# Block 1's channel-mixing MLP: upward products first, downward in seven products per pair, its gelu kept in memory, and a new order

## Chip, core and metric

One core of one Trainium2 chip runs the kernel. The metric is the device time of one execution in microseconds, the median of several runs. Before the change it was 502.88 us (three runs, 502.44 to 503.21). All data are float32; matrix operands are kept as two rounded parts, high and low (`hi`, `lo`), and a product is made of three matrix products: high by high, high by low, low by high.

## What is computed

The input `x` has 2048 rows of 512. It is normalised, goes through linear attention with 32 heads (`A`) and, separately, through a mixer block (`B`: a spatial-shift token mixer, then an MLP with 1376 hidden columns), and the result is `x + s * silu(B)`.

```python
def _A_ref(x, wqkv, wo):
    qkv = (x @ wqkv).reshape(B, S, 3, H, Dh).transpose(2, 0, 3, 1, 4)
    q, k, v = qkv[0], qkv[1], qkv[2]
    phi = lambda t: jnp.where(t > 0, t + 1, jnp.exp(t)) + 1e-6
    pq, pk = phi(q), phi(k)
    kv = jnp.einsum("bhsd,bhse->bhde", pk, v)
    z = jnp.einsum("bhsd->bhd", pk)
    num = jnp.einsum("bhqd,bhde->bhqe", pq, kv)
    den = jnp.einsum("bhqd,bhd->bhq", pq, z)[..., None] + 1e-6
    return (num / den).transpose(0, 2, 1, 3).reshape(B, S, D) @ wo

def _B_ref(x, w1, w2, w3, w4):
    h = _gelu(_layernorm(x) @ w1)
    g0 = jnp.pad(h[:, :, 0*c:1*c], ((0, 0), (1, 0), (0, 0)))[:, :S, :]
    ...
    x1 = x + jnp.concatenate([g0, g1, g2, g3], axis=-1) @ w2
    return x1 + _gelu(_layernorm(x1) @ w3) @ w4

xn = _layernorm(A_x)
return A_x + _A_ref(xn, A_wqkv, A_wo) * _silu(_B_ref(xn, B_w1, B_w2, B_w3, B_w4))
```

`g0` to `g3` are the quarters of `h`, shifted by +1, -1, +2 and -2 rows.

## The kernel before

**Tiles.** The 2048 rows are 16 tiles `i` of 128 rows, in four blocks `b` of four tiles (`QT = 4`). The hidden width 1376 is 11 pieces `f` of 128 columns, the last (`FB - 1`) of 96; the other ten go in five pairs `s` and `s + 5` (`NS = 5`).

**Seven products.** Where a product can be cut into 2 x 2 quarters, `seven` (and `down_late`) makes it of seven quarter products instead of eight, with sums and differences of quarters (`s1` to `s4` on the left, `t1` to `t4` on the right) as extra operands. The seven results are put together by evictions from PSUM: ScalarE copies one (`p1`, `p5`, `u2`), VectorE adds it to the next.

**The stages.** First key and query projections, the token mixer (`mix1`, `mix2`), and the sums of attention. Then, from about 225 us on, the MLP block by block. The upward product (by `w3`) with gelu is `up_last` and `up_pair` or `up_late`; the downward product (by `w4`) is `down` or `down_late`.

- *Blocks 0 and 1* go the plain way. `up_pair` writes the gelu twice, rounded and full, and VectorE makes the low part (`split`). `down` then adds, for each piece `f` and each of the four tiles `j`, three 512-wide products into the PSUM bank `acc{b}_{j}`. Upward and downward products of a block are woven together. `w4` is held for one block, and block 1 loads it again from memory (`load_w4`, tiles `w4_1_*`).
- *Blocks 2 and 3* are `LATE`. Their gelu stays in full in SBUF (`HF`, `HL`). After all upward products `down_forms` builds the left forms `a11, a12, s1, s2, s4, s3, a22` with their high and low parts, and `down_late` makes 7 products x 5 pairs x 3 terms of 256 columns for each of two tile pairs, and 4 x 3 for the last piece, against the right forms `W4F` (`wf`, `wu`), fetched by `fetch_w4`. The last block is `final`: its gates (`gate`) are cut finer, and its rows of `x1` are fetched ahead.

**Attention pairs.** `attends` works off tiles in pairs (`turn_q`, `forms_q`, `attend_pair`) at the points that the table `ATT` names, and leaves `so{i}` in SBUF until `gate(i)` uses it. `SUMS` names where the right forms of `w4` are built (`sums_w4`).

**What sets the order.** Every operation is recorded in a `Plan`, and `emit` then orders each engine's operations by due times that it works out, with a table of nudges (`SOONER`: operation number, quarter microseconds sooner) on top. SBUF tiles come from a pool `p` of 90 pieces of 2 KB a row; PSUM from `mm` (4 banks) and `acc` (4 banks). An operation that needs a tile waits for one to be free. Plain transfers are issued on SyncE's queue (`load`, `store`, `fetch`), accumulating ones on GpSimd's (`gather`); each queue works in order.

Of the kernel before, what the change touches and what calls it, by code (L numbers as in the profile page):

```python
# [11 lines left out]
ALU = mybir.AluOpType  # L12
AX = mybir.AxisListType

P = 128
# [381 lines left out]
def linear_attn_gated_by_mixer(  # L397
# [20 lines left out]
    QT = 4  # L418
# [6 lines left out]
    WARM = 3  # L425
    PIECE = BT + W
    EARLY = (), (10, 0, 5, 1, 6, 2)
    LATE = 2, 3
    SUMS = {(2, 2): (3,), (2, 3): (4,)}
    ATT = {(0, 4): (0,), (0, 5): (2,), (1, 2): (4,), (1, 3): (6,), (1, 4): (8,), (1, 5): (10,), (2, 1): (12,), (2, 3): (14,)}  # L430
    AHEAD = 100.0, 90.0, 70.0, 30.0, 10.0
    TH = BT // 2
    EDGE = 64
# [77 lines left out]
    g = nc.gpsimd  # L511
# [545 lines left out]
    GROUPS = ((0, 1), (2, 3), (4,))  # L1057
    HLEFT = (("a11", "a12"), ("s1", "s2"), ("s4", "s3"), ("a22",))
    QLEFT = (("a11", "a12"), ("a21", "a22"))
    TLEFT = (("t1", "t2"), ("t3", "t4"))  # L1060
    wtd = {}
    AF3, W4, YT, H3, HF, HL = {}, {}, {}, {}, {}, {}
# [186 lines left out]
    def up_last(b):  # L1249

        f, n = FB - 1, LASTW
        y = YT[b]
        ge = piece(f"gf{b}_{f}")
        late = b in LATE
        if late:
            HL[b] = ge.rows(n)
        else:
            hi, lo = rounds(f"f{b}_{f}")
        for t in range(2):
            h = t * TH, (t + 1) * TH  # L1260
            ps = bank(f"a{b}_{f}_{t}").cols(0, TH).rows(n)
            ks = y[f"b1{t + 1}"] + y[f"b2{t + 1}"]
            products(ps, [AF3["last"][c] + ks[c] for c in range(NC)])
            if not late:
                pl.act(hi.cols(*h).rows(n), ps, AF.Gelu_apprx_tanh)
            pl.act(ge.cols(*h).rows(n), ps, AF.Gelu_apprx_tanh)
        if late:
            return
        split(lo.rows(n), ge.rows(n), hi.rows(n))
        H3[b, f] = (hi, lo, n)  # L1270
# [20 lines left out]
    def up_late(b, s):  # L1291
        at = shelf(HF.setdefault(b, {}), f"h{b}_", QLEFT, "f")
        a11, a12, a21, a22 = (at(q, s)[0] for q in QS)
        ps = seven(f"{b}_{s}", (a11, a21, a22), lambda x, y: [AF3[s][x][c] + YT[b][y][c] for c in range(2)])
        for v in (a11, a21, a22):
            pl.act(v, v, AF.Gelu_apprx_tanh)
        pl.act(a12, ps, AF.Gelu_apprx_tanh)

    DF, LF = {}, {}

    def down_forms(b):

        full, rough = {}, {}
        at, fa = shelf(full, f"d{b}f_", HLEFT, "f"), shelf(rough, f"d{b}_", HLEFT)
        own = shelf(HF[b], f"h{b}_", QLEFT, "f")
        src = lambda q, g: wide(own, q, g)[0]
        w = lambda form, g: wide(at, form, g)[0]
        for form in ("a11", "a12", "s1", "s2", "s4", "s3", "a22"):
            for g in GROUPS:
                if form in ("s1", "s3"):  # L1310
                    pl.tt(w(form, g), src("a21", g), src("a22" if form == "s1" else "a11", g), ALU.add)
                elif form == "s2":
                    pl.tt(w("s2", g), w("s1", g), src("a11", g), ALU.add)
                elif form == "s4":
                    pl.tt(w("s4", g), w("s2", g), src("a12", g), ALU.add)
                v = src(form, g) if form[0] == "a" else w(form, g)
                hi, lo = wide(fa, form, g)
                rounded(hi, lo, v)
        DF[b] = {form: [fa(form, s) for s in range(NS)] for p in HLEFT for form in p}
        hi, lo = (v.rows(LASTW) for v in rounds(f"dl{b}"))  # L1320
        rounded(hi, lo, HL[b])
        LF[b] = hi, lo

# [379 lines left out]
    def attends(key):  # L1703
        for i in ATT.get(key, ()):
# [2 lines left out]
            forms_q(i)  # L1707
            attend_pair(i)
            for k in (i, i + 1):
                if k in XO:  # L1710
                    gate(k)

# [43 lines left out]
                gate(i)  # L1756
    fetch_w4()
    make_wl()
    for b in LATE:
        down_forms(b)  # L1760
        final = b == LATE[-1]
        if final:
            ahead(b)
            pl.patience = 0.0
        down_late(b, final)

    SOONER = (
# [42 lines left out]
    )  # L1810
    pl.emit(first=6.0, lead={"p": 9.0, "w": 20.0, "ab": 10.0}, reserve={"p": 8, "w": 1, "ab": 0}, window=9.0,
            ahead=6.0, table=SOONER)
# [39 lines left out]
```

## Time and profile before

| what | value |
|---|---|
| median of three runs | 502.88 us |
| the profiled execution's own time | 502.62 us |
| its span (first to last instruction) | 500.9 us |
| granted TensorE clock, mean | 1.000 |
| instructions | 9569 |
| HBM read, written | 72.47 MB, 36.06 MB |
| TensorE busy in the first 50 us | 48.82 us |
| first upward product of block 0, roughly | 225 us |
| first downward product of block 2, roughly | 440 us |
| last product | 496.3 us |

The profile is one execution. The busy shares are averages over stages. A row of the chain of waits gives start, length and what; a row of the stretches gives the busy time of each engine in it with the count of instructions; a group's row gives the number, the busy time and the mean of one in ns. In instruction rows `out<-in` are tile names; numbers at a tile's end count buffers.

### The profile page before, as it was taken

The numbers are of one execution on the slowest core, as the hardware profiler recorded it, in microseconds if no ns is written. First come the engines' busy times: TensorE is split into PE (matmuls) and PEld (weight loads), VectorE is DVE, ScalarE is ACT, GpSimd is POOL, SyncE is SP. The second block draws the span as 40 slices with busy tenths as digits, with TensorE's granted clock in tenths as the row PEclk, the third lists the DMA queues.
The fourth block names the chain that finished last, engine by engine and source line by source line (L and its number), as shares of the span: only waits on it lengthen the run. The fifth ranks groups of instructions, "written<-read, shape, count | busy, mean of one in ns | idle before, by whom it ended". The sixth has DMA issues, their size and how long they took to land.

```text
span 500.9 us, 9569 instructions
## 1 busy us (share of the span) xinstructions
PE 495.3 (99%) x3138; PEld 442.8 (88%) x3138; DVE 430.1 (86%) x850; ACT 368.0 (73%) x826; POOL 119.2 (24%) x208
## 2 busy tenths in 40 slices
PE   9999999999999999999999999999999999999996
PEld 6788778888888897899999989999989999999996
DVE  5998888789999958999899999978899785787983
ACT  5898999968696589999977855554657676856631
POOL 1384504438930232133100022000013100000320
PEclk9999999999999999999999999999999999999999
DMA  7968994999975899989978779975648937974674
GB/s 220 328 167 233 224 289 128 214 347 284 343 201 133 221 272 276 277 200 273 371 231 220 235 214 200 303 225 178 203 145 145 283 124 246 294 225 135 117 195 131
DMA packets 84345, 113.35 MB, mean 226 GB/s; under 512 B 10024, under 2 KB 37960, under 8 KB 84296
## 3 DMA queue, kind: packets, MB, share of 16 engines
q1 hardware_dynamic: 73640, 93.35, 57.2%
q0 software_dynamic: 10656, 19.40, 23.5%
q8 instruction: 24, 0.39, 0.3%
q14 instruction: 25, 0.20, 0.1%
HBM read 72.47 MB, written 36.06 MB: 217 GB/s over the span
## 4 chain that ended last, share of the span: by engine, by line
PE 94%; ACT 3%; DMA 1%; SPq 0%; DVE 0%; issue 0%; ACTq 0%
PE acc L146 12%; PE pb L146 11%; PE g L146 9%; PE h L146 9%; PE pbd L146 6%; PE pe L146 6%; PE pbx L146 5%; PE pbs L146 5%; PE pbm L146 5%; PE ped L146 3%; PE pa L146 3%; PE pex L146 3%; PE q L146 3%; PE pem L146 2%; PE pes L146 2%; PE a L146 2%
## 5 line engine op out<-in xcount | busy, mean ns | idle before, releaser
L225 POOL DMA_DIRECT2D xo<-x1d x12 | 10.6, 1067 | 186.7 <-DVE qz L201 112.6
L225 POOL DMA_DIRECT2D o<-xnd x16 | 14.0, 885 | 39.7 <-DMA w_s<-in_w 11.9
L225 POOL DMA_DIRECT2D zacc<-ke x12 | 12.3, 1028 | 31.9 <-DVE u_2l L191 9.9
L225 POOL DMA_DIRECT2D th<-in_x x14 | 12.1, 878 | 32.0 <-DVE th L201 14.3
L168 ACT ACTIVATE th<-xo 128x512 f32<-128x512 f32 (+1 forms) x16 | 9.7, 614 | 11.1 <-DVE xo L201 10.3
L225 POOL DMA_DIRECT2D xt<-nrow x16 | 15.1, 1441 | 6.0 <-DVE wt_01l L191 3.5
L191 DVE TENSOR_TENSOR ht<-h,abc 128x512 f32<-128x512 f32 x16 | 11.1, 691 | 5.6 <-PE h L146 5.4
L168 ACT ACTIVATE ht<-ht 128x512 f32<-128x512 f32 x16 | 9.9, 628 | 4.2 <-DVE ht L191 4.0
L168 ACT ACTIVATE p<-pe 128x256 f32<-128x256 f32 x20 | 7.6, 382 | 7.2 <-PE pe L146 7.1
L168 ACT ACTIVATE p<-pb 128x256 f32<-128x256 f32 x20 | 7.7, 383 | 7.2 <-PE pb L146 7.1
L196 POOL TENSOR_SCALAR w<-mv 128x4 f32<-128x4 f32 (+2 forms) x10 | 2.9, 289 | 40.0 <-ACT sq L168 39.7
L168 ACT ACTIVATE y<-o,nm,rs 128x512 f32<-128x512 f32 x16 | 12.0, 806 | 0.5 <-POOL nm L196 0.5
L168 ACT ACTIVATE u<-pb 128x256 f32<-128x256 f32 x20 | 7.7, 383 | 5.9 <-PE pb L146 5.8
L201 DVE SCALAR_TENSOR_TENSOR th<-th,so 128x512 f32<-128x512 f32 (+1 forms) x17 | 11.1, 652 | 0.8 <-ACT th L168 0.4
L168 ACT ACTIVATE sq<-o,mv 128x512 f32<-128x512 f32 x16 | 11.4, 719 | 0.1
L201 DVE SCALAR_TENSOR_TENSOR pq<-pq,rd 128x512 f32<-128x512 f32 x16 | 10.9, 682 | 0.3
L168 ACT ACTIVATE den<-den 128x32 f32<-128x32 f32 x16 | 3.6, 228 | 9.8 <-DVE den L1421 9.8
L201 DVE SCALAR_TENSOR_TENSOR qz<-pq,zb 128x512 f32<-128x512 f32 x16 | 10.8, 680 | 0.0
L168 ACT ACTIVATE gf<-gf 128x256 f32<-128x256 f32 (+1 forms) x20 | 10.5, 523 | 0.3
L1421 DVE TENSOR_REDUCE den<-qz 128x32 f32<-128x512 f32 x16 | 10.7, 676 | 0.1
L168 ACT ACTIVATE sq<-o 128x512 f32<-128x512 f32 x16 | 10.1, 630 | 0.1
L596 POOL TENSOR_TENSOR rs<-w,nhalf 128x4 f32<-128x4 f32 (+2 forms) x10 | 9.6, 962 | 0.7
(1974 smaller groups left out, 2383.5 us busy)
## 6 DMA issues: line engine op xcount, KB each, us to landing
w_s<-in_w SPq DMA_DIRECT2D x28, 256.0 KB, 5.8
x<-in_x SPq DMA_DIRECT2D x16, 256.0 KB, 5.1
xt<-in_xt SPq DMA_DIRECT2D x16, 256.0 KB, 5.7
xnd<-x SPq DMA_DIRECT2D x16, 256.0 KB, 6.0
xt<-nrow POOLq DMA_DIRECT2D x16, 256.0 KB, 8.2
pqd<-qr SPq DMA_DIRECT2D x16, 256.0 KB, 3.3
o<-xnd POOLq DMA_DIRECT2D x16, 256.0 KB, 6.0
x1d<-o SPq DMA_DIRECT2D x16, 256.0 KB, 5.8
```

Source lines behind the costliest of these rows:

```text
L146: lambda: nc.tensor.matmul(out.get(), lhs.get(), rhs.get(), start=start, stop=stop, skip_group_check=more))
L168: nc.scalar.activation(out.get(), src.get(), func, scale=get(scale), **kw)
L191: self.vec(eng, out, [a, b], lambda: self.e(eng).tensor_tensor(out.get(), a.get(), b.get(), op=op), True)
L196: lambda: self.e(eng).tensor_scalar(out.get(), a.get(), get(s1), get(s2), **kw), False,
L201: lambda: self.nc.vector.scalar_tensor_tensor(out.get(), a.get(), get(s), b.get(), op0=op0, op1=op1),
L225: lambda: self.nc.gpsimd.dma_start(out.get(), get(src), accum_op=ALU.add), mb=mb)
L596: lambda: g.tensor_tensor(out.get(), src.get(), nh.get(), op=ALU.pow))
L1421: pl.add("DVE", .6, .68, [t], [den], lambda: nc.vector.tensor_reduce(den.get(), t.get().rearrange("p (h d) -> p h d", d=DH), axis=AX.X, op ...
```

## The change

Block 1 joins the `LATE` blocks: its upward products run without the downward ones between them, and its downward product is made by `down_late`, after those of blocks 2 and 3 (`LINE = 2, 3, 1`), so that block 1 is now `final`. Since its full gelu does not stay in SBUF (`SPILL`), each finished pair of pieces is stored to memory (`hd`), as is its attention result (`sod`). `down_forms` fetches the forms `a11, a12, a22` back, and makes `s1` and `s3` by a fetch followed by an accumulating transfer of the second quarter, where blocks 2 and 3 use a VectorE addition. The reloads of `w4` for block 1 are gone. The attention pairs go at later points of the line of upward products, and the `SOONER` table is new.

```diff
-    LATE = 2, 3
-    SUMS = {(2, 2): (3,), (2, 3): (4,)}
-    ATT = {(0, 4): (0,), (0, 5): (2,), (1, 2): (4,), (1, 3): (6,), (1, 4): (8,), (1, 5): (10,), (2, 1): (12,), (2, 3): (14,)}
+    LATE = 1, 2, 3
+    SPILL = 1,
+    LINE = 2, 3, 1
+    SUMS = {(3, 1): (3,), (3, 3): (4,)}
+    ATT = {(0, 5): (0,), (1, 1): (2,), (1, 3): (4,), (2, 0): (6,), (2, 2): (8,), (2, 4): (10,), (3, 1): (12,), (3, 3): (14,)}
...
+    HN = {(q, g): 2 * k + g for k, q in enumerate(("a11", "a12", "a21", "a22")) for g in range(2)}
+    HN.update({p: 8 + k for k, p in enumerate(QLEFT)})
+    hd = {b: memory(f"hd{b}", 11 * 512) for b in SPILL}
+    sod = {i: memory(f"sod{i}") for b in SPILL for i in range(b * QT, b * QT + QT)}
...
         if late:
+            if b in SPILL:
+                put(b, 10, HL[b], n)
             return
...
         pl.act(a12, ps, AF.Gelu_apprx_tanh)
+        if b in SPILL and (s % 2 or s == NS - 1):
+            for key in [(q, s // 2) for q in QS] if s < NS - 1 else QLEFT:
+                put(b, HN[key], HF[b][key][0])
+
+    def put(b, n, v, rows=P):
+        op = pl.store(hd[b][:rows, n * 512:(n + 1) * 512], v)
+        op.patience = 10.0
+        pl.soon(op)
+
+    def slab(b, q, g):
+        if len(g) > 1:
+            n = HN[q, g[0] // 2] * 512
+            return hd[b][:, n:n + 512]
+        p = next(p for p in QLEFT if q in p)
+        o = HN[p] * 512 + p.index(q) * TH
+        return hd[b][:, o:o + TH]
...
         for form in ("a11", "a12", "s1", "s2", "s4", "s3", "a22"):
             for g in GROUPS:
                 if form in ("s1", "s3"):
-                    pl.tt(w(form, g), src("a21", g), src("a22" if form == "s1" else "a11", g), ALU.add)
+                    other = "a22" if form == "s1" else "a11"
+                    if spilled:
+                        pl.fetch(w(form, g), slab(b, "a21", g))
+                        pl.gather(w(form, g), slab(b, other, g))
+                    else:
+                        pl.tt(w(form, g), src("a21", g), src(other, g), ALU.add)
...
+                elif spilled:
+                    pl.fetch(src(form, g), slab(b, form, g))
...
+        if spilled:
+            HL[b] = piece(f"hl{b}").rows(LASTW)
+            pl.fetch(HL[b], hd[b][:LASTW, 10 * 512:11 * 512])
...
             for k in (i, i + 1):
+                if k // QT in SPILL:
+                    pl.soon(pl.store(sod[k].all, SO[k]))
...
-    for b in LATE:
+    for b in LINE:
         down_forms(b)
-        final = b == LATE[-1]
+        final = b == LINE[-1]
+        if b in SPILL:
+            for i in range(b * QT, b * QT + QT):
+                SO[i] = piece(f"sb{i}")
+                pl.fetch(SO[i], sod[i].all)
...
     SOONER = (
-        15, 27, 20, 21, 26, 2, 30, 3, 36, 10, 52, 1, 82, 2, 91, 2, 99, 4, 103, 12, 112, -14, 113, -2, 124, 10,
+        23, 8, 39, 7, 48, -50, 69, 53, 90, 10, 93, 21, 96, 20, 97, 12, 99, 9, 106, -6, 118, -9, 120, 6, 124, 8,
...
```

How the order moves, at three places. On TensorE before, inside block 1 (`acc1_*`: its downward banks; `w4_1_*`: its copy of `w4`; `f1_*`: its gelu; `pe1_1`: an upward product of its pair 1):

```order
L146 MATMUL acc1_1_4398<-w4_1_0l_4129,f1_0h_4330 128x512
L146 MATMUL acc1_1_4398<-w4_1_0h_4097,f1_0l_4400 128x512
L146 MATMUL acc1_1_4398<-w4_1_5h_4179,f1_5h_4396 128x512
L146 MATMUL acc1_3_4276<-w4_1_0l_4129,f1_0h_4330 128x512
L146 MATMUL acc1_3_4276<-w4_1_0h_4097,f1_0l_4400 128x512
L146 MATMUL acc1_1_4398<-w4_1_5l_4162,f1_5h_4396 128x512
L146 MATMUL pe1_1_4406<-yt11h_4164,w3_1_s0l_2538 128x256
L146 MATMUL acc1_2_4304<-w4_1_5h_4179,f1_5h_4396 128x512
L146 MATMUL acc1_2_4304<-w4_1_5l_4162,f1_5h_4396 128x512
```

and in the changed kernel, near the end, where block 3's last downward products (`pbd3*`) meet block 1's first (`pbd10`, `pad10`, `ped10`; `d1_*`: its left forms; `wf_*`, `wu_*`: right forms):

```order
L146 MATMUL pbd30_6533<-w4_l1h_6366,dl3h_6524 128x256
L146 MATMUL pbd30_6533<-w4_l1l_6386,dl3h_6524 128x256
L146 MATMUL pbd30_6533<-w4_l1h_6366,dl3l_6541 128x256
L146 MATMUL pbd10_6978<-wf_b111h_5829,d1_a111l_6871 128x256
L146 MATMUL pbd31_6621<-w4_l1l_6386,dl3h_6524 128x256
L146 MATMUL pbd31_6621<-w4_l1h_6366,dl3l_6541 128x256
L146 MATMUL pad10_6996<-wf_b210l_6019,d1_a120h_6954 128x256
L146 MATMUL ped10_7047<-wu_00h_6070,d1_s10h_6898 128x256
L146 MATMUL ped10_7047<-wu_00l_6079,d1_s10h_6898 128x256
L146 MATMUL ped10_7047<-wu_00h_6070,d1_s10l_6909 128x256
```

The 512-wide products of block 1 among its upward ones are gone, and 256-wide ones stand behind block 3's.

On VectorE, around the first eviction of block 1's upward stage; before (`gf1_*`: gelu input of block 1; `so`, `th`: gates of block 0; `f1_*l`: low parts; `qz`, `den`: attention):

```order
L191 TENSOR_TENSOR so2_4064<-so2_4064,xo2_4198 128x512
L191 TENSOR_TENSOR so3_4113<-so3_4113,xo3_4210 128x512
L201 SCALAR_TENSOR_TENSOR th2_4346<-th2_4346,so2_4064 128x512
L191 TENSOR_TENSOR gf1_5_4375<-pb1_0_4251,p51_0_4297 128x256
L201 SCALAR_TENSOR_TENSOR th3_4361<-th3_4361,so3_4113 128x512
L201 SCALAR_TENSOR_TENSOR qz6_4390<-pq6_4147,zb_2155 128x512
L191 TENSOR_TENSOR f1_0l_4400<-gf1_0_4279,f1_0h_4330 128x512
L1421 TENSOR_REDUCE den6_4410<-qz6_4390 128x32
L201 SCALAR_TENSOR_TENSOR qz7_4418<-pq7_4175,zb_2155 128x512
L1424 RECIPROCAL rd6_4426<-den6_4410 128x32
```

and in the changed kernel (`h1_*`: quarters of block 1's gelu, `q2*`, `pq5`: attention pairs):

```order
L191 TENSOR_TENSOR h1_a220f_4247<-pb1_0_4173,p51_0_4210 128x256
L191 TENSOR_TENSOR h1_a210f_4251<-u21_0_4223,pe1_0_4156 128x256
L191 TENSOR_TENSOR q2l_4261<-q2t_4115,q2h_4245 128x512
L191 TENSOR_TENSOR h1_a110f_4201<-pa1_1_4253,p11_1_4198 128x256
L191 TENSOR_TENSOR q2f0_4274<-q3t_4085 128x256
L201 SCALAR_TENSOR_TENSOR th1_4167<-th1_4167,so1_3983 128x512
L1459 RECIPROCAL rd5_4292<-den5_4218 128x32
L191 TENSOR_TENSOR q2f0_4274<-q2f0_4274,q2t_4115 128x256
L191 TENSOR_TENSOR h1_a220f_4247<-pb1_1_4165,p51_1_4296 128x256
L201 SCALAR_TENSOR_TENSOR pq5_4012<-pq5_4012,rd5_4292 128x512
L191 TENSOR_TENSOR q2f1_4321<-q2t_4115,q3t_4085 128x256
```

The low parts `f1_*l` of block 1 are gone from its upward stage, and operations of attention pairs stand between the evictions.

On GpSimd's queue, in the last part; before (`xo`: rows of `x1` added to the downward result; `th`: rows of `x` added to the gate):

```order
L225 DMA xo9_6558<-x1d9_3146 128x512
L225 DMA th8_6791<-in_x 128x512
L225 DMA xo10_6768<-x1d10_3072 128x512
L225 DMA xo11_6784<-x1d11_3118 128x512
L225 DMA th9_6847<-in_x 128x512
L225 DMA th10_6913<-in_x 128x512
L225 DMA th12_7027<-in_x 128x512
L225 DMA th11_6979<-in_x 128x512
L225 DMA th14_7095<-in_x 128x512
```

and in the changed kernel (`d1f_*`: the sums `s1`, `s3` of block 1's forms, from the spilled gelu `hd1`):

```order
L225 DMA d1f_s10f_6588<-hd1_4178 128x512
L225 DMA th10_6696<-in_x 128x512
L225 DMA th11_6735<-in_x 128x512
L225 DMA d1f_s1xf_6708<-hd1_4178 128x256
L225 DMA d1f_s11f_6711<-hd1_4178 128x512
L225 DMA d1f_s30f_6732<-hd1_4178 128x512
L225 DMA xo13_6756<-x1d13_3308 128x512
L225 DMA xo12_6666<-x1d12_3170 128x512
L225 DMA d1f_s31f_6833<-hd1_4178 128x512
L225 DMA d1f_s4xf_6862<-hd1_4178 128x256
L225 DMA xo14_6959<-x1d14_3245 128x512
L225 DMA xo15_6934<-x1d15_3438 128x512
```

Six accumulating transfers for block 1's forms stand among those for the gates of blocks 2 and 3, and block 3's rows `xo12` to `xo15` are added on this queue too.

More of the change, by code (lines that the diff above doesn't have):

```diff
@@ L1297, in up_late @@
         pl.act(a12, ps, AF.Gelu_apprx_tanh)
+        if b in SPILL and (s % 2 or s == NS - 1):
[12 more added lines that the diff above has]
+        return hd[b][:, o:o + TH]
     DF, LF = {}, {}
     def down_forms(b):
-        full, rough = {}, {}
+        full, rough, back = {}, {}, {}
         at, fa = shelf(full, f"d{b}f_", HLEFT, "f"), shelf(rough, f"d{b}_", HLEFT)
-        own = shelf(HF[b], f"h{b}_", QLEFT, "f")
+        spilled = b in SPILL
+        own = shelf(back if spilled else HF[b], f"h{b}_" + "b" * spilled, QLEFT, "f")
         src = lambda q, g: wide(own, q, g)[0]
```

88 rows, old and new, of the table SOONER are left out of this document.

## The prediction

> **What bounds the kernel now.** I read the page first: busy times, slices, share of the chain that ended last.
>
> ```profile
> PE 495.3 (99%) x3138; PEld 442.8 (88%) x3138; DVE 430.1 (86%) x850; ACT 368.0 (73%) x826; POOL 119.2 (24%) x208
> DVE  5998888789999958999899999978899785787983
> DMA  7968994999975899989978779975648937974674
> PE 94%; ACT 3%; DMA 1%; SPq 0%; DVE 0%; issue 0%; ACTq 0%
> ```
>
> The chain is TensorE for 94%. VectorE is next with 86%, and its slices touch 9 for long stretches, so it is the engine to fear. Then busy time by stretches, cut at the stages from the start of block 0's upward products:
>
> ```profile
> 228.00:295.00 67.00, 67.00 (x446) 61.26 (x445) 64.55 (x127) 54.03 (x130) 5.49 (x10) 1.00 0.87 270
> 301.30:440.10 138.80, 138.78 (x1044) 132.59 (x1044) 117.27 (x239) 86.82 (x217) 10.50 (x12) 1.00 0.76 214
> 412.00:440.10 28.10, 28.10 (x240) 28.10 (x239) 19.50 (x41) 20.65 (x54) 0.00 (x0) 1.00 0.81 258
> 440.10:496.60 56.50, 56.50 (x477) 56.30 (x475) 44.52 (x90) 27.90 (x57) 8.63 (x10) 1.00 0.65 162
> ```
>
> Columns: PE, PEld, DVE, ACT, POOL busy with counts, granted clock, DMA share, GB/s. TensorE lacks 0.02 us in these 262 us, at clock 1.00. A busy TensorE need not be at its peak, so the spacing of products decides, from the chain in order of time (start, length, what):
>
> ```profile
> 132.73 9.01 PE h L146 x39
> 461.99 5.45 PE pbd L146 x46
> 494.22 2.41 PE pbd L146 x20
> 496.65 0.39 ACT th L168
> 497.06 0.44 DVE th L201
> 497.52 0.42 DVE th L191
> ```
>
> A 512-wide product takes 9.01/39 = 0.231 us, a 256-wide one 5.45/46 = 0.1185 us. A second price for the narrow one comes from a stretch that holds nothing else:
>
> ```profile
> 440.00:470.00 30.00, 30.00 (x255) 30.00 (x254) 24.40 (x49) 19.52 (x42) 3.36 (x4) 1.00 0.56 152
> ```
>
> 30.00/255 = 0.1176 us. They follow one another without gaps: the time is the sum of the products, plus a start and an end. The end is the chain's last rows: an activation, two VectorE operations and the store behind the last product.
>
> **The products.** Removed: block 1's downward products into `acc`, 11 pieces of F x 4 row tiles x 3 terms = 132 of 512 columns, 132 x 0.231 = 30.5 us. Added: seven forms x 5 slabs x 3 terms x 2 row pairs = 210, and for the piece of 96 rows 4 x 3 x 2 = 24: 234 of 256 columns, 27.5 us at 0.1176 or 27.7 us at 0.1185. The instruction order bears this out: 512-wide products go from 1006 to 874, 256-wide from 1984 to 2218. Gain 2.8 to 3.0 us; I take 2.8, the price from the downward products themselves. Upward products, attention and everything ahead keep their counts. The tail, `gate` behind the last product, is unchanged code, now for row tile 7 instead of 15.
>
> A rule that speaks against the change: the Trainium skill, TensorE: Matmul & The Clock Gate, section Back-to-back issue gap, has the spacing set by the weight load and the product together, 131 ns at 512 columns and 81 ns at 128. Halfway by width that would be some 98 ns at 256 (an estimate from that page), three quarters of the wide one, and trading 132 wide for 234 narrow products would lose 10 us. The trace disagrees here: 0.1176 against 0.231 is 0.51.
>
> **VectorE and ScalarE.** Durations of one, from the groups by line:
>
> ```profile
> L191 DVE TENSOR_TENSOR w_al<-w_s,w_ah 128x512 fp32r<-128x512 f32 x5 | 3.4, 685 | 0.0
> L191 DVE TENSOR_TENSOR gf<-pa,p 128x256 f32<-128x256 f32 x10 | 4.2, 416 | 0.0
> L168 ACT ACTIVATE w_ah<-w_s 128x512 fp32r<-128x512 f32 x5 | 3.1, 631 | 0.0
> L168 ACT ACTIVATE p<-pb 128x256 f32<-128x256 f32 x20 | 7.7, 383 | 7.2 <-PE pb L146 7.1
> ```
>
> Block 1 loses ten 512-wide splits, a second gelu each, and four products with `so`; it gains the seven forms' splits, the sums s2 and s4 and the evictions of `down_late`. Net by the order: VectorE +4 of 512 and +15 of 256, 4 x 0.685 + 15 x 0.416 = 9.0 us; ScalarE +15 of 256 less one smaller, 5.5 us. Both fit in idle time overall; where they fall matters. Between the first eviction of block 1's upward stage and the last of block 3's there were 239 VectorE operations, 117.27 us, in 138.8 us. Now there are 228, at 117.27/239 = 0.491 us each 111.9 us, but the `acc` products no longer stand between, so TensorE needs only 980 x 0.1176 + 3 x 0.231 = 115.9 us for that stretch: VectorE would be 97% busy there, against 84%. I cost this at nothing, because VectorE has kept such a share without TensorE losing anything:
>
> ```profile
> 260.00:290.00 30.00, 30.00 (x211) 27.77 (x210) 29.39 (x61) 22.97 (x50) 0.00 (x0) 1.00 0.79 229
> 290.00:320.00 30.00, 30.00 (x193) 27.16 (x193) 29.36 (x56) 18.00 (x43) 7.05 (x8) 1.00 0.90 233
> ```
>
> 98% for 60 us. If that cover is gone, it is the second rival below. Behind it, in three downward blocks, there are 129 VectorE operations at 44.52/90 = 0.495 us = 64 us in 722 x 0.1176 = 85 us: room.
>
> **Transfers.** Queue totals and landing times:
>
> ```profile
> q1 hardware_dynamic: 73640, 93.35, 57.2%
> q0 software_dynamic: 10656, 19.40, 23.5%
> w_5h<-w4d SPq DMA_DIRECT2D x2, 256.0 KB
> xo<-x1d SPq DMA_DIRECT2D x4, 256.0 KB, 3.5
> xo<-x1d POOLq DMA_DIRECT2D x12, 256.0 KB, 5.6
> out<-th SPq DMA_DIRECT2D x15, 256.0 KB, 2.9
> ```
>
> 57.2% of 500.9 us for 93.35 MB is 0.80 us of all 16 engines per 256 KB on SP's queue; the same for POOL's accumulating queue is 1.59 us. In the upward stages 22 reloads of `w4` go (21.5 x 0.80 = 17 us) and 11 spills of gelu and 4 of attention come (14.75 x 0.80 = 12 us): lighter. In the tail come 17.25 fetches (forms, last piece, `sb`: 13.8 us) and 5 slabs of accumulating sums in six transfers (8.0 us); block 1's gates move there too, in all 8 more ordinary accumulating transfers (12.7 us) and 4 stores (3.2 us): 37.7 us. From the first `wf` fetch to the end the share was 0.81 x 28.1 + 0.65 x 56.5 = 59.5 us in 84.6; now about 97 us in 84.6 + 27.5 = 112 us, a share of 0.87. Block 0's stretch (0.87, above) bore as much without a wait. Cost nothing.
>
> SP is passed by more issues, 458 to 471 transfers. Stores of spills wait on SP for a gelu, and behind them stand the fetches for attention pairs. On POOL six sums `d1f` stand between transfers that wait for gates. A sum of block 1's form was one VectorE operation (0.685 us); now it is a fetch, then an accumulating transfer: 3.5 + 5.6 = 9.1 us. They are issued while block 3's downward products, 234 x 0.1176 = 27.5 us, still run. No row of before shows such a pair with a consumer behind it: below it costs nothing, above the transfer, copy and split stand bare, 5.6 + 0.63 + 0.685 = 6.9 us. I take nothing, since the cover is three times the 9.1 us.
>
> **Sum.** The profiled execution took 502.62 us (span 500.9), 502.62 - 2.8 = 499.8 us; the median of the runs shown is 0.26 above it, so 502.88 - 2.8 = **500.1 us**.
>
> **Rivals.** *Half the gain lost:* VectorE reaches 94.5% in blocks 1 to 3: 111.9/0.945 = 118.4, 2.5 us over the 115.9, so 502.6 us. *VectorE becomes the bound, slower than before:* upward and attention products share the four `mm` banks, and with no `acc` products to fill in, TensorE waits for evictions that are queued behind attention's work. The break-even is 111.9/(115.9 + 2.8) = 94.3%; at 92% the stretch takes 121.6 us, +5.7, in all 505.8 us. For it: attention's pairs, moved later, now lie wholly there. Against it: 98% from 260 to 320. *Tail transfers late:* a sum behind `xo13` or `th10` on POOL lands after its turn; from 3.8 us of waiting it is slower, at 6.9 us 507.0. For it: POOL waits in order. Against: 27.5 us of cover. *Narrow products dearer,* bound by their weight loads:
>
> ```profile
> L146 PEld LDWEIGHTS pbd<-wf_b11xl,d_a11xh x4: 187/187/188, 441.1 to 478.6; 128*128 128x128 f32 x4
> ```
>
> at 0.187 us each, 234 take 43.8 against 30.5, +13.3, 516.2 us. The 0.1176 spacing with these same loads speaks against it. The Trainium skill, TensorE: Matmul & The Clock Gate, section Back-to-back issue gap, names this mechanism; it hangs by that row. That the change doesn't do what it says is excluded by the counts.
>
> **Chances.** Forecast 0.62; half the gain lost 0.13; VectorE the bound 0.14; tail 0.09; narrow products 0.02. A measurement of this kernel tells about 0.2%, 1.0 us, from no change. Faster 0.62, the same 0.13, slower 0.25. The likeliest case alone spans 499.3 (gain 3.0, and 0.6 us less at the start, whose order is new too) to 501.5. The range runs 499.3 to 505.8: it takes in the half gain and half of the bound case.
>
> **What would show it.** Right: 132 wide products fewer, spacing 0.231 and 0.118 as before; TensorE gapless through the upward blocks with VectorE at 95% or more; the last product about 2.8 us earlier; `d1f` sums landed before their copies start. Wrong: idle time of TensorE ended by VectorE or ScalarE in blocks 1 to 3, or by `d1` forms at block 1's downward start; TensorE short of its span by over 2 us past 200 us.

## The result, and the profile after

The changed kernel takes 505.45 us (median of 15 runs, 503.05 to 508.6), the kernel before on the same chip 502.88 us: ratio 1.0055, 95% interval 1.0034 to 1.0077. It is slower by about 2.6 us where 2.8 us less were forecast. The profiled execution took 506.13 us, with a span of 504.4 us. One run further below, of `u2_first` (513.92 us), was a slow one: it stands in that kernel's median, not in its ratio.

Of the page after: busy time by engine, VectorE's slices, shares of the chain that ended last.

```profile
PE 495.1 (98%) x3240; PEld 446.8 (89%) x3240; DVE 436.9 (87%) x869; ACT 370.6 (73%) x840; POOL 124.1 (25%) x214
DVE  4998768699889967999899999999999789795973
PE 89%; DMA 5%; DVE 3%; ACT 2%; SPq 1%; issue 0%; DVEq 0%; ACTq 0%
```

There are 102 products more, as costed (132 fewer, 234 more). But the chain leaves TensorE for 11% of the span (6% before), and DMA holds 5% of it (1% before).

Stretches of the MLP after: blocks 1 to 3 upward in two parts, then the three downward blocks (columns as in the prediction).

```profile
305.30:365.00 59.70, 59.70 (x503) 59.52 (x502) 59.12 (x127) 39.02 (x103) 3.43 (x4) 1.00 0.78 227
365.00:422.00 57.00, 56.72 (x475) 56.29 (x474) 51.89 (x110) 42.53 (x108) 0.00 (x0) 1.00 0.62 197
422.00:500.40 78.40, 78.33 (x657) 77.72 (x655) 59.47 (x119) 38.91 (x80) 20.89 (x24) 1.00 0.93 240
```

VectorE is busy for 99% of the first 60 us and TensorE still lacks nothing; in all three TensorE is idle for 0.35 us. The bulk of the loss is not there. Three stretches of the beginning, before:

```profile
0.00:12.50 12.50, 11.40 (x36) 7.73 (x37) 6.58 (x14) 7.00 (x16) 1.33 (x9) 1.00 0.78 220
62.00:75.00 13.00, 13.00 (x57) 10.20 (x57) 11.24 (x23) 12.95 (x24) 0.86 (x1) 1.00 1.04 286
75.00:87.50 12.50, 12.50 (x56) 10.04 (x55) 10.44 (x18) 12.35 (x30) 5.31 (x9) 1.00 0.46 129
```

and after:

```profile
0.00:12.50 12.50, 10.37 (x32) 6.96 (x33) 6.03 (x13) 6.69 (x15) 1.33 (x9) 1.00 0.75 217
62.00:75.00 13.00, 10.21 (x42) 7.70 (x41) 9.14 (x19) 9.50 (x17) 1.37 (x2) 0.97 1.04 257
75.00:87.50 12.50, 12.50 (x50) 9.92 (x49) 10.85 (x18) 11.60 (x27) 2.08 (x3) 0.89 0.46 133
```

From 62 to 87.5 us there were 113 products, now 92: TensorE idles 2.8 us, and behind that its granted clock is 0.89. This is in the first projections of block 2, more than 130 us ahead of the first product that the change of the MLP touches.

**The whole account.** I take the first product of the MLP (the first into a bank `a`, by the last piece of `w3`) and the last product of all, in each timeline. Before:

```profile
225.25 0.28 PE L146 MATMUL a<-yb110h,w_lh 128*96 128x256 f32 x1
...
496.33 0.28 PE L146 MATMUL pbd<-w_l1h,dl3l 96*128 96x256 f32 x1
```

After:

```profile
231.54 0.28 PE L146 MATMUL a<-yb110h,w_lh 128*96 128x256 f32 x1
...
500.12 0.28 PE L146 MATMUL pbd<-w_l1h,dl1l 96*128 96x256 f32 x1
```

The first MLP product comes 6.29 us later, the MLP is 2.50 us shorter (271.08 to 268.58), and what follows the last product is 0.29 us shorter: 6.29 - 2.50 - 0.29 = 3.50, the growth of the span. To part products from gaps I took each product's time from its start to the next start, less 0.1177 us for 256 columns, 0.2305 for 512 and 0.06 for 128, and summed that over all products. This excess, the time lost, is 11.6 us before and 17.2 us after ahead of the MLP, and 2.5 and 3.6 us inside it. Of the 5.6 us more ahead of it, 0.9 fall in the first 12.5 us and 4.7 between 62 and 87.5 us. The products' own time is 0.7 us more ahead of the MLP and 3.6 less inside it: 2.9 us less in all, as forecast.

### The profile page after: what moved, and what is told of

It reads as the page before. It is cut to its first block, busy times and chain, and to the rows that moved or that the text cites. A ratio compares the mean times of both kernels' runs of the same rounds, so it can differ in the third digit from the quotient of the medians.

```text
span 504.4 us, 9873 instructions
## 1 busy us (share of the span) xinstructions
PE 495.1 (98%) x3240; PEld 446.8 (89%) x3240; DVE 436.9 (87%) x869; ACT 370.6 (73%) x840; POOL 124.1 (25%) x214
## 4 chain that ended last, share of the span: by engine, by line
PE 89%; DMA 5%; DVE 3%; ACT 2%; SPq 1%; issue 0%; DVEq 0%; ACTq 0%
PE pb L146 9%; PE pbd L146 9%; PE h L146 9%; PE g L146 8%; PE acc L146 6%; PE pbx L146 5%; PE pe L146 5%; PE pbm L146 5%; PE ped L146 5%; PE pbs L146 4%; PE q L146 3%; PE k L146 3%; PE pex L146 3%; PE pad L146 3%; PE pem L146 2%; PE pa L146 2%
## 5 line engine op out<-in xcount | busy, mean ns | idle before, releaser
L196 POOL TENSOR_SCALAR w<-mv 128x4 f32<-128x4 f32 (+2 forms) x10 | 4.4, 440 | 36.0 <-ACT sq L168 35.6
L168 ACT ACTIVATE x<-x,nm,rs 128x512 f32<-128x512 f32 x12 | 9.0, 805 | 0.0
L201 DVE SCALAR_TENSOR_TENSOR th<-th,so 128x512 f32<-128x512 f32 x12 | 8.1, 680 | 0.6 <-ACT th L168 0.5
L168 ACT ACTIVATE sq<-x,mv 128x512 f32<-128x512 f32 x12 | 8.5, 710 | 0.0
```

The costliest lines, as they stand in the source:

```text
L168: nc.scalar.activation(out.get(), src.get(), func, scale=get(scale), **kw)
L196: lambda: self.e(eng).tensor_scalar(out.get(), a.get(), get(s1), get(s2), **kw), False,
L201: lambda: self.nc.vector.scalar_tensor_tensor(out.get(), a.get(), get(s), b.get(), op0=op0, op1=op1),
```

## Why block 2's projections wait

What TensorE waited for from 62 to 90 us, after (total, times, longest):

```profile
PE pax L146 <- DVE u_2l L191: 2.3, 1, 2.3
PE pax L146 <- ACT u_2h L168: 0.5, 1, 0.5
```

`u_2` is the third quarter of block 2's centred, transposed `x`, in its high and low parts. VectorE's timeline shows why its low part came late:

```profile
67.14 0.69 DVE L191 TENSOR_TENSOR u_0l<-xt,u_0h 128x512 fp32r<-128x512 f32 x1 [0.33 <-ACT u_0h L168]
68.90 0.69 DVE L191 TENSOR_TENSOR u_1l<-xt,u_1h 128x512 fp32r<-128x512 f32 x1 [1.07 <-ACT u_1h L168]
70.30 0.42 DVE L191 TENSOR_TENSOR xf<-xt,xt 128x256 f32<-128x256 f32 x1 [0.70 <-DMA xt<-nrow]
72.47 0.42 DVE L191 TENSOR_TENSOR xf<-xt,xt 128x256 f32<-128x256 f32 x1 [1.75 <-DMA xt<-nrow]
72.82 0.75 DVE L191 TENSOR_TENSOR xf<-xf,xt 128x256 f32<-128x256 f32 x2
73.49 0.68 DVE L191 TENSOR_TENSOR u_2l<-xt,u_2h 128x512 fp32r<-128x512 f32 x1
```

The four accumulating transfers `xt<-nrow` land one after another. The sums `xf` need the fourth, at 72.47 us, and `u_2l` stands behind them. The transfers themselves are late. POOL issues them when a 2 KB row, `nrow`, has reached memory, and SP stores that row. Before, POOL's row, then SP's, and the median time of the four transfers from issue to landing:

```profile
56.66 3.54 POOL L225 DMA_DIRECT2D xt<-nrow  x4 [2.50 <-PE pax L146]
...
54.07 0.26 SPq L212 DMA_DIRECT2D nrow<-ar  x1
...
55.32 0.34 SPq L212 DMA_DIRECT2D pqd<-qr  x1
...
56.74 1.01 SPq L207 DMA_DIRECT2D x<-in_x  x2
...
xt<-nrow POOLq DMA_DIRECT2D x4, 256.0 KB, 7.9
```

After:

```profile
58.94 3.54 POOL L225 DMA_DIRECT2D xt<-nrow  x4 [4.23 <-DMA nrow<-ar]
...
53.18 0.33 SPq L212 DMA_DIRECT2D pqd<-qr  x1
53.60 1.63 SPq L212 DMA_DIRECT2D xnd<-x  x2
55.32 0.71 SPq L212 DMA_DIRECT2D nrow<-ar  x1
...
58.69 1.78 SPq L207 DMA_DIRECT2D x<-in_x  x4
...
xt<-nrow POOLq DMA_DIRECT2D x4, 256.0 KB, 9.5
```

Now a `pqd` and two `xnd` stores of 256 KB pass the row, which is issued 1.25 us later. The semaphore of the row's store tells when it landed: before at 56.14 us, 2.1 us after its issue, now at 58.65 us, 3.3 us after it. It is the row that POOL waited for before, too, though the profile names a product, `PE pax`, as what ended that wait: the gathers start 0.5 us behind the landing, just as in the run `row_first` below (56.81 to 57.34 us), where the profile names the row. They start 2.3 us later now, and four loads of 256 KB stand beside them, where two did. They also take longer: the fourth gather, the one that the sums need, landed at 67.7 us before and lands at 72.5 us now, 4.8 us later.

## The experiments

In the experiments the planner is left out: the order and the buffers that it chose were recorded from each program and are emitted as a list, so that single operations can move while all others stay.

```diff
-    pl.emit(first=6.0, lead={"p": 9.0, "w": 20.0, "ab": 10.0}, ...
+    pl.emit(SEQUENCE, PLACES)
```

Medians with 95% intervals of the ratio to the kernel before, which took 502.53 to 502.77 us beside them:

| kernel | us | ratio | interval |
|---|---|---|---|
| after_again | 504.54 | 1.0043 | 1.0026 to 1.0059 |
| fb_ma | 514.47 | 1.0237 | 1.0222 to 1.0252 |
| fa_mb | 522.97 | 1.0422 | 1.0407 to 1.0438 |
| u2_first | 505.89 | 1.0082 | 1.0044 to 1.0121 |
| early_before | 501.75 | 0.9980 | 0.9958 to 1.0002 |
| early_after | 505.29 | 1.0070 | 1.0044 to 1.0096 |
| row_first | 502.27 | 1.0005 | 0.9987 to 1.0023 |
| row_first_x_late | 501.50 | 0.9984 | 0.9972 to 0.9997 |
| before_row_late | 504.10 | 1.0032 | 1.0020 to 1.0043 |
| mended_old | 503.16 | 1.0018 | 1.0006 to 1.0029 |
| start_row_x | 500.61 | 0.9959 | 0.9940 to 0.9978 |
| tail_early | 499.63 | 0.9945 | 0.9932 to 0.9959 |

**The changed kernel again.** No edit.

> The changed kernel as it is. Front theory (the time was lost ahead of the MLP, in the order that was made anew there: VectorE's u_2l of block 2 stands behind sums that wait for a later transfer, TensorE idles 3 us near 71 to 75 us and its granted clock falls behind that): 504.5 to 506.5 us, and the profile shows again a wait of 1.5 to 3 us of the first-layer products for u_2l and a granted clock under 0.98 in 75 to 100 us. MLP theory (the loss is in the upward stage, whose VectorE share is near 100 %, or in the tail's transfers): the same time, but the wait before 75 us may be absent while the time stays; then the front was not it.

As the front theory has it: TensorE waited 2.0 us for `u_2l`, and the granted clock was 0.87 from 75 to 87.5 us.

**Two orders joined at the first MLP product.** `SEQUENCE` is one kernel's up to there and the other's from there on.

> The kernel before's order up to the first upward product of the MLP, the changed kernel's MLP behind it. Front theory: the 502.88 of before less the 2.8 us of products, plus at most 1 us of small spacings in the MLP: 500.0 to 501.2 us, the wait for u_2l near 74 us gone and the clock at 1.00 in 75 to 100 us. MLP theory: 504.5 to 506 us, no better than the changed kernel.

> The changed kernel's order up to the first upward product of the MLP, the kernel before's MLP behind it (block 1 downward by whole products, nothing spilled). Front theory: before's 502.88 plus the 5.5 us that the front lost: 507 to 509 us. MLP theory: 502.4 to 503.5 us, as before.

Both missed every expected time. The join cost more than what it was to test: `fb_ma` loses 16.9 us between 150 and 262.5 us (by the account above), against 4.2 us in each of the two kernels that it is made of, since the two orders hold other buffers and have other transfers under way at that place. The times tell nothing of the change. One part of the profiles does, and as the front theory has it: with the order of before, the beginning of `fb_ma` has its 113 products between 62 and 87.5 us, at a granted clock of 1.00; with the changed order, `fa_mb` waits 2.1 us for `u_2l` there.

**Only VectorE's order.**

```diff
 u_1l<-xt_1,u_1h
+u_2l<-xt_2,u_2h
 xf_0<-xt_0,xt_2
 xf_0<-xt_1,xt_3
+u_3l<-xt_3,u_3h
 xf_1<-xf_0,xt_0
 xf_1<-xf_0,xt_1
-u_2l<-xt_2,u_2h
 xf_3<-xf_1,xt_2
 xf_3<-xf_1,xt_3
-u_3l<-xt_3,u_3h
```

> The changed kernel with two VectorE instructions moved: u_2l of block 2 ahead of the four sums xf that wait for its fourth transfer, u_3l ahead of two of them. Front theory: the 2.3 us wait for u_2l is gone and the lowered clock behind it too: 501 to 503.5 us. Transfer theory (the late transfers xt<-nrow are the cause, and the order of VectorE only names the wait): the wait moves to u_3l and 504.5 to 505.5 us stay. MLP theory: 505.4 us, no change.

The front theory in its first form, that VectorE's order was the cause, fell. `u_2l` is no longer waited for, but the wait goes to other operands, as the transfer theory has it, though mostly not to the one that it named (`u_3l`):

```profile
PE pex L146 <- ACT xs_0h L168: 1.8, 1, 1.8
PE pax L146 <- ACT u_3h L168: 0.4, 1, 0.4
```

`xs_0` is made from the sums of all four quarters. What is late is the transfers; VectorE's order only names the wait.

**Joined at 90 us instead,** where the two orders hold nearly the same buffers.

> The kernel before's order for everything that its plan puts into the first 90 us (all engines), the changed kernel's order from there on. Front theory: the changed kernel's 505.4 less the 0.9 us at its start and the 5.0 us of 62 to 100 us: 499.0 to 501.0 us, no wait for block 2's operands near 74 us. MLP theory: 504.5 to 506 us. Cut theory (joining two orders itself costs, as the 514.5 and 523.0 of the joins at 229 us showed): over 503 us with waits of more than 1 us of TensorE between 85 and 130 us.

> The converse: the changed kernel's order for the first 90 us, the kernel before's from there on, MLP and all. Front theory: 502.7 plus about 5 us: 507 to 509 us, with the wait of 2 us for u_2l near 72 us. MLP theory: 502.4 to 503.5 us, as before.

`early_before` lost the wait and came to 501.75 us, 2.8 to 3.7 us better than the changed kernel with the same MLP, though above the expected range; its MLP lost 4.6 us by spacing. `early_after` has the old MLP and is slower than before all the same, by 2.8 us instead of the 5 expected: TensorE's stall is there (1.7 us of idle time), without the lowered clock.

```profile
62.00:75.00 13.00, 11.33 (x48) 8.48 (x47) 10.58 (x21) 10.90 (x20) 2.31 (x3) 1.00 1.05 274
75.00:87.50 12.50, 12.50 (x54) 10.05 (x55) 9.82 (x17) 12.50 (x30) 2.41 (x4) 1.00 0.62 175
```

**SP's queue.** Row store first; and, in the second kernel, the four loads later as well.

```diff
+nrow<-ar
 pqd<-qr
 xnd<-x
 xnd<-x
-nrow<-ar
...
-x<-in_x    (four of them)
 xnd<-x
 xnd<-x
 pqd<-qr
 xnd<-x
+x<-in_x    (four of them)
```

> The changed kernel with one move on SP's queue: the 2 KB store of block 2's row of norms (nrow<-ar) goes ahead of one pqd store and two xnd stores of 256 KB instead of behind them. Transfer theory (block 2's gathers xt<-nrow come late because the row's store lands 3.6 us after its issue behind 768 KB, and the wait only changes its name, u_2l or xs_0h): POOL's wait for nrow<-ar ends 1.5 to 2.5 us earlier, TensorE's stall of 62 to 87 us falls from 5.0 to 2 to 3.5 us, 502.5 to 504 us. Rival (the gathers are slow by the other loads beside them, not late in their issue): stall and time as they were, 504.5 to 505.5 us.

> As row_first, and also the four loads x<-in_x of 256 KB that stand together ahead of the gathers' landings go behind the next three xnd stores and a pqd store of SP's queue. Transfer theory with both causes: the gathers land 3 to 4 us earlier than in the changed kernel, the stall of 62 to 87 us is under 1 us, 500.0 to 502 us. If only the issue mattered: as row_first. If the loads that are now later starve what needs them: a new wait for x12 to x15 of 1 us or more behind 75 us.

The row alone gave 2.3 to 3.2 us (against 504.54 and 505.45), slightly more than expected; the granted clock is 1.00 again, and 1.5 us are still lost between 62 and 87.5 us by the account above. With the loads later that stall is gone as well (0.3 us). The 0.8 us between the two medians, whose intervals just overlap, go the same way:

```profile
57.06 3.54 POOL L225 DMA_DIRECT2D xt<-nrow  x4 [3.08 <-DMA nrow<-ar]
```

```profile
62.00:75.00 13.00, 13.00 (x58) 10.43 (x57) 12.57 (x25) 12.96 (x24) 0.86 (x1) 1.00 1.03 275
75.00:87.50 12.50, 12.50 (x56) 9.94 (x55) 8.89 (x15) 12.41 (x31) 4.75 (x9) 1.00 0.55 172
```

**The same in the kernel before.** Its MLP and all engines but SP as they were; the row store goes behind one `pqd` and one `xnd` store, and the four loads stand together.

```diff
-nrow<-ar
 arow<-ar
 pqd<-qr
 xnd<-x
+nrow<-ar
 x<-in_x
 x<-in_x
+x<-in_x
+x<-in_x
```

> The kernel before, unchanged but for SP's queue: block 2's 2 KB row store goes behind one pqd store and one xnd store, and its four loads x<-in_x stand together, as in the changed kernel. Transfer theory: the same stall arises without any change of the MLP: gathers issued 2 to 3 us later than at 56.66 us, TensorE waits 1.5 to 3 us for block 2's operands between 66 and 76 us, 504 to 506 us. Rival (the stall comes from the changed kernel's order on VectorE or ScalarE): 502.4 to 503 us.

It became slower by 1.3 us (504.10 against 502.77; 1.6 by the ratio), in the expected range, though the parts were smaller than expected: the row landed at 57.84 us instead of 56.14, the gathers went from 56.66 to 58.40 us, by 1.7 us where 2 to 3 were expected, and TensorE was idle for 0.7 us where 1.5 to 3 were. It had 106 products between 62 and 87.5 us instead of 113.

```profile
58.40 3.55 POOL L225 DMA_DIRECT2D xt<-nrow  x4 [5.16 <-PE pbx L146]
```

```profile
62.00:75.00 13.00, 12.27 (x50) 8.81 (x49) 9.85 (x20) 11.82 (x21) 1.71 (x2) 1.00 1.05 253
75.00:87.50 12.50, 12.50 (x56) 9.98 (x56) 10.73 (x20) 12.32 (x31) 4.50 (x7) 1.00 0.49 147
```

So such an order of SP makes a stall in either kernel, here a smaller one behind two stores instead of three; the MLP has no part in it. All fourteen profiles agree: where the fourth gather landed by 68.1 us (seven profiles), 0.2 to 0.4 us were lost between 62 and 87.5 us; where it landed at 69.5 (`before_row_late`) and 69.8 us (`row_first`), 1.9 and 1.5; where it landed from 71.2 us on (the other five), 2.5 to 5.1.

**The MLP alone.** The mended beginning of `row_first_x_late` to 90 us, then the order of before with its MLP.

> The order of row_first_x_late for the first 90 us, the kernel before's order and its MLP from there on: what the MLP's change is worth behind one and the same, undisturbed beginning. By the profiles so far the stage from the first product of the MLP on takes 271.1 us with the old MLP and 266.9 to 269.6 with the new one, with 0.7 us more of products ahead of it: the new MLP gains 2.1 us of the 2.9 us of products, less what its waits on spilled transfers give back, and this kernel comes to 501.5 + 1.5 to 2.5 = 503.0 to 504.0 us. If the new MLP gave its whole gain back: 501.2 to 502.0 us.

503.16 us against 501.50: behind one and the same beginning the new MLP is worth 1.7 us, also by the two ratios to the kernel before.

**The start.** The order of before for the first 18 us, too; on SP it has

```diff
 xt_0<-in_xt
-xt_1<-in_xt
 wk_s<-in_wqkv
+xt_1<-in_xt
 wk_s<-in_wqkv
```

> row_first_x_late with the kernel before's order for the first 18 us of the plan as well. In the profiles the changed kernel's first 12.5 us lose 5.5 to 6.0 us beyond the products' own time, the kernel before's 4.5 to 4.8, by its weight load wk_1 that stands one place later on SP. Start theory: the gain adds to the other: 501.5 less 0.8 to 1.0 us, 500.4 to 500.8 us, loss of the first 12.5 us 4.5 to 4.9 us. Rival (the later first products let block 0's operands come in time; earlier ones only wait later): 501.3 to 501.7 us, with 0.7 us or more of new waits between 12 and 60 us.

Its median is 0.9 us lower, as expected, but the two intervals overlap, so the times alone do not show it. The profiles do: by the account the eight with the changed start lose 5.5 to 6.0 us in the first 12.5 us, the six with the start of before 4.5 to 4.8. The profiled execution of `start_row_x` was the slowest of its runs, 504.97 us, and shows a cost that I had put at nothing. ScalarE's timeline, tail:

```profile
460.89 0.42 ACT L168 ACTIVATE d_a11xh<-h_ba11xf 128x256 fp32r<-128x256 f32 x1 [1.21 <-DMA h_ba11xf<-hd]
...
462.58 0.42 ACT L168 ACTIVATE d_a11xh<-h_ba11xf 128x256 fp32r<-128x256 f32 x1 [0.76 <-DMA h_ba11xf<-hd]
464.45 0.63 ACT L168 ACTIVATE d_a121h<-h_ba121f 128x512 fp32r<-128x512 f32 x1 [1.45 <-DMA h_ba121f<-hd]
```

The evictions `xo`, which empty TensorE's banks, stand behind these pieces in the order of ScalarE and VectorE, so a late piece of the spilled gelu holds them up, and TensorE waits for a bank. Its longest waits in this stretch, and the stretch:

```profile
PE pbd L146 <- DVE xo L201: 1.1, 2, 0.9
455.00:475.00 20.00, 18.64 (x150) 17.83 (x150) 12.60 (x26) 9.94 (x22) 6.75 (x8) 1.00 1.05 278
```

**The fetches of the tail earlier.**

```diff
 d1f_s11f<-hd
+h_ba11xf<-hd    (two of them)
+h_ba121f<-hd
 xo<-x1d
 d1f_s30f<-hd
 out<-th
-h_ba11xf<-hd    (two of them)
-h_ba121f<-hd
```

> start_row_x with three of the downward stage's reads of spilled pieces (h_ba11xf twice, h_ba121f) issued ahead of xo<-x1d, d1f_s30f and an out store on SP instead of behind them, some 1 to 2 us earlier. Theory that the spilled pieces arrive just in time and at times late (in the profile of start_row_x ScalarE waited 1.2, 0.8 and 1.4 us for them at 461 to 464 us, and TensorE lost 2.5 us at 462 to 475 us): ScalarE's waits for these three fall under 0.5 us each, TensorE loses under 0.5 us between 455 and 475 us, 499.9 to 500.6 us. Rival (that loss was a disturbance of one execution and no matter of the order): 500.6 us and no change, or up to 0.5 us more if xo<-x1d and d1f_s30f are now the late ones.

In the profile the three waits are gone, and the same stage (4 us earlier now) has 171 products in 20 us instead of 150:

```profile
455.55 0.41 ACT L168 ACTIVATE d_a11xh<-h_ba11xf 128x256 fp32r<-128x256 f32 x1
...
456.38 0.41 ACT L168 ACTIVATE d_a11xh<-h_ba11xf 128x256 fp32r<-128x256 f32 x1
456.69 0.62 ACT L168 ACTIVATE d_a121h<-h_ba121f 128x512 fp32r<-128x512 f32 x1
```

```profile
451.00:471.00 20.00, 20.00 (x171) 20.00 (x170) 14.65 (x29) 11.18 (x24) 6.90 (x8) 1.00 1.10 286
```

At 499.63 us (498.73 to 501.13) this is the fastest of all: 2.9 us under the kernel before, 5.8 under the changed one. But what this last edit is worth is not shown. The intervals of `tail_early` and `start_row_x` overlap. The profile of `start_row_x` also lost 3.8 us near 128 us, where `tail_early` lost 0.1 with the same order. And `u2_first`, `row_first` and `row_first_x_late`, which have the old order of these fetches, had 170 or 171 products in the same 20 us, too. So the rival that I had named, a disturbance of one execution, is not ruled out.

## Why the prediction was wrong

**The step that failed** is the sentence "Upward products, attention and everything ahead keep their counts", with "0.6 us less at the start, whose order is new too" as all that a new order could do. The counts were kept, the time was not: 5.6 us more were lost ahead of the MLP. The diff named a new table of nudges for all operations, and I read its effect only where the MLP changed. The order of SP around `nrow<-ar` was to be had beforehand: its row of 2 KB is passed by three stores of 256 KB. Moving five issues on SP (`row_first_x_late`: the row and four loads) brings 3.0 to 4.0 us, and a like order made in the kernel before costs it 1.3. With the start of before as well, the kernel comes to 500.61 us, half a microsecond from the forecast of 500.1. That the measured 505.45 us lies inside the range of 499.3 to 505.8 is luck: the range reached so far for the sake of the VectorE rival, which did not come.

**The products** were right: 0.1177 and 0.2305 us as costed, 2.9 us less in all.

**VectorE at nothing** was right in the changed kernel, but for 0.6 us. It was busy for 99% from 305 to 365 us with TensorE gapless. Both rivals that live on VectorE fell: they needed 2.5 and 5.7 us in this stage, where what TensorE lost to late evictions came to 0.6 us in `after` and to 1.6 at most (`early_before`); most of these evictions were late behind transfers, as told next.

**Transfers at nothing** was mis-sized. The time lost inside the MLP, by the account above:

| profile | MLP, first to last product | lost in it |
|---|---|---|
| old MLP: before, early_after, mended_old, before_row_late | 271.0 to 271.1 | 2.4 to 2.5 |
| new MLP: u2_first, tail_early, row_first | 266.9 to 267.7 | 1.9 to 2.7 |
| new MLP: row_first_x_late, after, after_again | 268.4 to 268.7 | 3.4 to 3.7 |
| new MLP: early_before, start_row_x | 269.6, 270.0 | 4.6, 5.0 |

The old MLP repeats within 0.1 us; the new one varies by 3 us between profiles, and gives back up to 2.5 of its 2.9 us. In the profiles that lost most, the loss sits in three places, and at each an engine waits for a plain transfer first. About 139 us behind the first MLP product ScalarE waits for `q13d<-q13z`, a transfer of an attention pair; about 181 us behind it VectorE waits for `wt<-wt_40h`, of the sums of `w4`. Both stand in the upward stage, where `ATT` and `SUMS` put them anew. In `early_before`:

```profile
364.37 0.63 ACT L168 ACTIVATE q10s1h<-q10f 128x512 fp32r<-128x512 f32 x1 [0.82 <-DMA q13d<-q13z]
DVE wt L191 <- DMA wt<-wt_40h: 1.2, 1, 1.2
```

In `u2_first`, which has neither wait, TensorE loses 0.1 us around each; in `early_before`, `after`, `after_again` and `row_first_x_late` 0.6 to 1.2. The third place is the tail. There ScalarE waits for spilled pieces in every profile of the new MLP, 1.5 to 6.0 us in all, but only in `start_row_x`, with the most, did TensorE lose much there (2.5 us more than with the old MLP); elsewhere it was 0.6 us more at most.

So the cover of "three times the 9.1 us" held for the sums `d1f`, which no engine waited for; it was plain transfers, which I had not followed to their consumers, that came late. The rival "tail transfers late" (507.0) named the third place, but the wrong transfers, and sized it for 6.9 us. Why the same transfers come in time in one execution and late in another is left open.

**Narrow products dearer** fell, as its row said.

## What to carry to other kernels

A change that makes an order anew is a change everywhere: compare the orders of all stages, above all the small stores and loads that many others wait for, before adding up the stage that was meant. When a wait moves to another operand as soon as the one named is served, look at what feeds them all. A transfer that is covered by time has still to be followed to the engine that takes it in, and to what stands behind it there. And one clean profile behind an edit proves little where kernels without the edit have clean ones too.

## What the runs showed of the hardware

- From issue to landing, by its semaphore, the 2 KB row took 1.7 to 2.1 us in `before_row_late`, `before`, `row_first` and `row_first_x_late`. Behind the `pqd` and the two `xnd` stores it took 3.3 us in `after` and 2.9 in `after_again`, but 2.4 in `u2_first`, 2.2 in `early_after` and 2.0 in `fa_mb`. In `before`, too, three `xnd` stores had gone ahead of it. So the landing need not be slower behind large stores; the later issue is what the changed order has in common.
- Accumulating transfers of 256 KB took a median of 7.9 us to land in `before` and 9.5 in `after`, where four plain loads of 256 KB, not two, were issued beside them; the slowest took 9.2 and 11.7 us.
- Behind the stall near 73 us the granted clock fell in three of the five profiles that have the changed kernel's order there (`after`, `after_again`, `u2_first`: 0.89, 0.87 and 0.89 from 75 to 87.5 us). In the first it was 0.65 for 4.5 us, with 14 products where 19 fit:

```profile
74.50:79.00 4.50, 4.50 (x14) 3.54 (x14) 4.29 (x9) 3.60 (x7) 0.87 (x1) 0.65 0.71 168
```

  Total idle time does not tell the cases apart: `fa_mb` stayed at 1.00 with 2.2 us of it, as `early_after` did with 1.7, while `after_again` fell with 2.1. The clock records in the traces do. Each change falls on a grid of 3.41 us (the clock was 1.00 for 68.27 us, 20 steps, then 0.50 for 3.41 us in all three). I cut each trace by its own grid and took TensorE's idle time in each step that ran at 1.00. Where it was 1.91 us or more the next step ran at 0.50: 2.40, 1.96 and 1.94 us in the three profiles above, 1.96 in `start_row_x` at 127 us, 1.91 in `fb_ma` at 199 us and a whole step in `fa_mb` at 201 us. Where it was 1.65 us or less the clock stayed at 1.00: 1.65 in `fa_mb`, whose 2.2 us lie across two steps, 1.57 in `early_after`, 1.60 in `fb_ma` at 260 us. No step fell between, so in these traces the border lies between 1.65 and 1.91 us of 3.41; that it is the idle time of the step that decides is inferred.
- The time of one kernel varies between executions by more than that of the kernel before, which in 29 runs on one chip lay between 501.74 and 503.68 us. Kernels with the spill: 498.88 to 504.97 us in seven runs of `start_row_x`, 499.33 to 505.25 in twelve of `early_before`, but 498.73 to 501.13 in six of `tail_early`. Without it: 504.41 to 508.74 in six of `early_after`. So the spill alone is not what makes the spread.
